# Four transformer blocks on one core: the first two tiles of x in one load, the first weights on one queue in halves, and five instruction lists put in a new order

## The chip, the cores and the metric

The kernel runs on one core of a Trainium2 chip. The metric is the device time of one execution in microseconds. Before the change three runs took 328.64, 327.99 and 327.65 us; the median is 327.99.

A core has a matrix engine (PE), three engines for elementwise work (DVE, the vector engine; ACT, the scalar engine; POOL, GpSimd) and a queue engine (SP) that only starts transfers here. PE multiplies a weight tile of 128x128 with a moving tile of up to 512 columns and writes to PSUM, of which there are eight banks of 128x512 float32. The engines run their own instruction streams and wait for each other on semaphores.

## The reference

x has 2048 rows of 512 columns. Two kinds of block follow each other twice:

```python
def _A_ref(x, wqkv, wo):                # H = 32 heads of Dh = 16
    qkv = (x @ wqkv).reshape(B, S, 3, H, Dh).transpose(2, 0, 3, 1, 4)
    q, k, v = qkv[0], qkv[1], qkv[2]
    phi = lambda t: jnp.where(t > 0, t + 1, jnp.exp(t)) + 1e-6
    pq, pk = phi(q), phi(k)
    kv = jnp.einsum("bhsd,bhse->bhde", pk, v)
    z = jnp.einsum("bhsd->bhd", pk)
    num = jnp.einsum("bhqd,bhde->bhqe", pq, kv)
    den = jnp.einsum("bhqd,bhd->bhq", pq, z)[..., None] + 1e-6
    return (num / den).transpose(0, 2, 1, 3).reshape(B, S, D) @ wo

def _B_ref(x, w1, b1, w2, b2):          # F = 1792
    y = _layernorm(x)
    h = _gelu(jnp.einsum("bsd,df->bsf", y, w1) + b1)
    return jnp.einsum("bsf,fd->bsd", h, w2) + b2

x = x + _A_ref(_layernorm(x), wqkv, wo)
x = x + _B_ref(_layernorm(x), w1, b1, w2, b2)
x = x + _A_ref(_layernorm(x), wqkv, wo)
x = x + _B_ref(_layernorm(x), w1, b1, w2, b2)
```

The attention is linear: kv and z are sums over all rows, so no row's output can be made before all rows' K have been seen.

## The kernel before

**Tiles and chunks.** The rows are cut into 16 tiles of 128 rows and 4 chunks of four tiles. In the first attention the chunks are taken in the order 3, 0, 1, 2, so the first tiles are 12 and 13. All weights stay in SBUF.

**Names.** The kernel builds a graph of operations, each of which is one or a few instructions, and every operation has a name made of its kind, the layer (0 or 1), and the tile or chunk. For a tile of x: `stats`, `aggr`, `veps`, `pow`, `nmr` and `norm` are the steps of the layernorm (for the very first tiles `cen` subtracts the mean and `ysc` scales later, and tile 13 takes its sum and its sum of squares on ACT: `sumA0_13`, `sqA0_13`, `negA0_13`, L722 to L731). The normalized tile is transposed, either on PE (`PT`, L797, with a copy `tc` from PSUM, L807) or by a transposing DMA that SP starts (`TA` and `TB`, L784; `TP`, L1069, for the attention's output). `K` (L852) and `Q` (L870, L883) are the projections, `phik` and `phiq` their feature map, which is made of `exp`, `relu` and `min`. `G` (L953, L985) sums phi(k) times the normalized rows, `Z` sums phi(k); `gt` and `ga` collect G from PSUM on DVE, and from it `KV` (L1008) makes kv and `M` (L1031) joins it with wo. `D` (L1077) gives the denominators, then come `den`, `rec` and the product `pr` (L1065). `WO` (L1101) is the output projection, `RA` (L1106) its residual add. `W1` (L1133) with `gelu` (L1139) on ACT and `W2` (L1171, the last tile in two halves at L1158) are the two matrices of the second block, `RB` (L1177, L1181) its residual add, `OD` (L1183, L1165) the store of a tile of the result. `W10_1_3_0` is W1 in layer 0, chunk 1, third block of 128 of the 1792 features, first part.

**What sets the order.** Each engine plays a list of operation names that is written out in the configuration: 388 names for PE, 323 for ACT, 506 for DVE, 220 for POOL, 104 for SP. Which engine does an operation is fixed in another table. A planner, `Scheduler.run`, replays the five lists with modelled durations: from its times it takes only which buffer slot or PSUM bank a tile gets, and with that which semaphores an operation waits for. It does not change the order in a list. An operation whose inputs are late holds up all that stands behind it in its engine's list; this holds for SP too, where a transpose that waits for its tile holds up the transposes and stores behind it.

**The loads at the start.** SP starts, in this order, `x0` (128 KB, tile 12, L648), `x1` (128 KB, tile 13, L650), `wk0` (the upper half of the K weights, 256 KB, L657), `x2` (256 KB, tiles 14 and 15, L650), `wq` (512 KB, L660) and the three other chunks of x (`xc0` to `xc2`, 512 KB each, L644). ACT starts `wk1`, the lower half of the K weights, as the first operation of its list. POOL starts the loads of wv, wo, w1 and w2 in pieces of up to 896 KB later on, in places of its own list. Behind x and wk come the first matmuls: PE transposes tile 12 and tile 13, with dummy matmuls (L690) before and between, and does `K0_12` and `K0_13`, then tile 14's transpose and the first Q projection `Q0_3_0`.

Of the kernel before, what the change touches and what calls it, by code (L numbers as in the profile page):

```python
# [7 lines left out]
ACT = mybir.ActivationFunctionType  # L8
ALU = mybir.AluOpType

P = 128
# [16 lines left out]
DMA_LAT = 800.0  # L28

# [81 lines left out]
class Scheduler:  # L111
# [12 lines left out]
    def run(self):  # L124
# [13 lines left out]
        bus = 0.0  # L138
        for _ in g.ops:
            best = None  # L140
            for e in ENGINES:
                if len(self.order[e]) == len(queue[e]):
                    continue
                o = queue[e][len(self.order[e])]
                if o.missing:
                    continue
                at = max(o.ready, free[e])
                if o.table is not None and o.table != table:
                    at = max(o.ready, free[e] + TABLE_LOAD)
                slots = [self.slot_time(t) for t in o.tiles if t.slot is None]  # L150
# [20 lines left out]
            if o.fast:  # L171
                dve_busy = at + dur
            if e == "pool" and o.sem is None and o.dur > 300.0:
                dur += max(0.0, min(dve_busy - at, 400.0))
                pool_busy = at + dur
# [92 lines left out]
def assign_waits(graph, order, sems, dma_sems):  # L268
# [10 lines left out]
    while len(done) < total:  # L279
        moved = False  # L280
        for e in ENGINES:
# [43 lines left out]
    N_WARM2=1, N_IDLE=[4, 3], XQ='sp', WKQ='sp act', WK1=1,  # L325
    LAND={'x0': 3210, 'x1': 3930, 'wk1': 5300, 'wk0': 6430, 'x2': 6950, 'wq': 8450, 'xc0': 9730, 'xc1': 11020, 'xc2': 12240},
# [1041 lines left out]
```

## Time and profile before

| what | us |
|---|---|
| median of three runs | 327.99 |
| the profiled execution, first to last instruction | 326.2 |
| PE busy | 320.6 |
| DVE busy | 218.7 |
| ACT busy | 197.5 |
| POOL busy | 131.2 |
| x0, x1, wk1, wk0, x2, wq landed at | 3.18, 4.76, 5.53, 6.24, 6.94, 8.41 |

The profile gives the profiled execution from its first to its last instruction only: 326.2 us, which is 1.8 us less than the median of the timed runs. A matmul's busy time covers its way through the array, in which the next one already starts, so the busy time of PE hides some pauses of a few tenths; they are seen in the starts of the instructions and in the waits of the weight loads (PEld). Chain lines say what the end hung on, step by step backwards. A row of the timeline has a start, a duration, the engine, the line, and in square brackets the idle time before it with what ended it. A stretch row has the busy time of each engine with its number of instructions, the granted clock, the share of the DMA engines and the rate in GB/s.

### The profile page before, as it was taken

Reading aid. Unit: us, or ns where it says so; the run is one execution under the profiler, and the core shown is the slowest. Engines: PE = TensorE matmul, PEld = TensorE weight load, DVE = VectorE, ACT = ScalarE, POOL = GpSimd, SP = SyncE. Lnnn points to the kernel's source line nnn. Section 1 sums busy time; section 2 is a strip of 40 time slices with the busy share of each in tenths; the row PEclk is TensorE's granted clock in tenths of the full one; section 3 lists DMA queues with packets and bytes.
Section 4 is the critical chain, followed back from the end, with each engine's and each line's share of the span. In section 5 each row is a group of like instructions: output and inputs, shape, how many; then the busy total and the mean of one; then the engine's idle time right before and its main releaser. Section 6 shows DMA issues by size and latency. Waiting matters only on the chain.

```text
span 326.2 us, 4796 instructions
## 1 busy us (share of the span) xinstructions
PE 320.6 (98%) x1724; PEld 158.2 (48%) x1724; DVE 218.7 (67%) x506; ACT 197.5 (61%) x338; POOL 131.2 (40%) x224
## 2 busy tenths in 40 slices
PE   7999999999999999999999999999999999999996
PEld 3444545656544444444444444458644444444453
DVE  4998689989866662535468899999988663300132
ACT  5998889744753387357963395969923553645200
POOL 3465637673238106134139525645811275100000
PEclk9999999999999999999999999999999999999999
DMA  7424662524012400312110200111153233300011
GB/s 239 163 51 92 173 223 62 181 49 81 21 31 48 97 1 2 74 22 55 27 32 19 47 17 0 28 39 36 32 92 72 48 45 69 81 0 2 32 64 50
DMA packets 47028, 20.39 MB, mean 62 GB/s; under 512 B 41948, under 2 KB 45532, under 8 KB 47004
## 3 DMA queue, kind: packets, MB, share of 16 engines
q1 hardware_dynamic: 45676, 15.09, 20.4%
q0 software_dynamic: 1056, 4.72, 4.5%
q10 hardware_dynamic: 272, 0.26, 0.3%
q8 instruction: 14, 0.23, 0.3%
q14 instruction: 10, 0.08, 0.1%
HBM read 8.00 MB, written 2.10 MB: 31 GB/s over the span
## 4 chain that ended last, share of the span: by engine, by line
PE 91%; DVE 4%; DMA 2%; ACT 1%; SPq 1%; issue 1%; ACTq 0%
PE ps L1133 29%; PE ps L1171 26%; PE ps L1101 9%; PE ps L852 9%; PE ps L870 5%; PE ps L953 4%; PE ps L883 3%; PE ps L985 2%; DMA t<-in_A_x_dram 1%; PE ps L1158 1%; DMA t<-yb 1%; DVE t L839 1%; PE ps L1008 1%; PE ps L1077 1%; PE ps L797 1%
## 5 line engine op out<-in xcount | busy, mean ns | idle before, releaser
L1139 ACT ACTIVATE gT<-ps,b1c 128x512 bf16<-128x512 f32 (+1 forms) x140 | 76.9, 601 | 61.2 <-PE ps L1133 60.8
L1133 PE MATMUL ps<-t,w 128*128 128x512 bf16 (+1 forms) x560 | 102.2, 336 | 0.5 <-DMA t<-yb 0.3
L1171 PE MATMUL ps<-w,gT 128*128 128x512 bf16 x434 | 97.3, 379 | 0.0
L1133 PEld LDWEIGHTS ps<-t,w 128*128 128x128 bf16 x560 | 54.4, 98 | 44.5 <-DMA t<-yb 0.7
L1171 PEld LDWEIGHTS ps<-w,gT 128*128 128x128 bf16 x434 | 42.4, 98 | 50.4 <-ACT gT L1139 0.3
L822 ACT ACTIVATE eb<-ps 128x512 bf16<-128x512 f32 x56 | 32.1, 606 | 21.3 <-PE ps L852 20.3
L749 POOL TENSOR_TENSOR rstd<-veps,neghalf 128x1 f32<-128x1 f32 x64 | 36.7, 581 | 8.2 <-DVE veps L747 5.5
L1181 DVE TENSOR_TENSOR outb<-ps,xsb 128x512 bf16<-128x512 f32 x15 | 10.3, 689 | 40.3 <-PE ps L1171 32.1
L734 DVE BATCH_NORM_STATS2 stats<-xsb 128x6 f32<-128x512 f32 x48 | 32.0, 681 | 0.2
L1101 PE MATMUL ps<-gtb,t 128*128 128x512 bf16 x128 | 31.8, 379 | 0.1
L852 PE MATMUL ps<-wqkv,t 128*128 128x512 bf16 x128 | 31.1, 379 | 0.0
L769 ACT ACTIVATE yb<-xsb,nmr,rstd 128x512 bf16<-128x512 f32 x21 | 16.8, 811 | 12.6 <-POOL nmr L766 12.5
L833 ACT ACTIVATE rb<-ps 128x512 bf16<-128x512 f32 x38 | 22.3, 611 | 1.6 <-PE ps L852 0.9
L739 POOL TENSOR_SCALAR veps<-mv 128x1 f32<-128x1 f32 x32 | 7.3, 227 | 38.4 <-DVE mv L736 36.6
L774 DVE TENSOR_SCALAR yb<-xsb,mv,rstd 128x512 bf16<-128x512 f32 x27 | 15.0, 572 | 9.0 <-POOL rstd L749 8.9
L835 DVE TENSOR_SCALAR eb<-eb 128x512 bf16<-128x512 bf16 x46 | 13.6, 306 | 10.9 <-ACT eb L822 10.8
L1118 POOL TENSOR_TENSOR xsb<-xsb,b2b 128x512 f32<-128x512 f32 x14 | 17.0, 1218 | 8.1 <-DVE yb L774 6.5
L870 PE MATMUL ps<-wqkv,t 128*128 128x512 bf16 x80 | 20.2, 379 | 0.0
L747 POOL TENSOR_SCALAR veps<-mv 128x1 f32<-128x1 f32 x28 | 8.4, 305 | 28.0 <-DVE mv L736 26.9
L1101 PEld LDWEIGHTS ps<-gtb,t 128*128 128x128 bf16 x128 | 12.3, 98 | 14.9 <-ACT gtb L966 0.7
L852 PEld LDWEIGHTS ps<-wqkv,t 128*128 128x128 bf16 x128 | 12.0, 97 | 14.7 <-ACT t L807 0.9
L1065 POOL TENSOR_TENSOR t<-t,rr 128x512 bf16<-128x512 bf16 x7 | 7.7, 1100 | 24.4 <-DVE rr L1061 14.1
(103 smaller groups left out, 398.7 us busy)
## 6 DMA issues: line engine op xcount, KB each, us to landing
w<-in_B_w_dram POOLq DMA_DIRECT2D x4, 896.0 KB, 5.9
out_dram<-outb SPq DMA_DIRECT2D x15, 128.0 KB, 2.1
t<-in_A_x_dram SPq DMA_DIRECT2D x3, 512.0 KB, 7.3
t<-yb SPq DMA_TRANSPOSE x56, 2.5
wqkv<-in_A_wqkv_dram SPq DMA_DIRECT2D x1, 512.0 KB, 5.7
wo<-in_A_wo_dram POOLq DMA_DIRECT2D x1, 512.0 KB, 6.6
wqkv<-in_A_wqkv_dram POOLq DMA_DIRECT2D x1, 512.0 KB, 4.5
t<-t SPq DMA_TRANSPOSE x20, 2.5
```

The costliest lines, as they stand in the source:

```text
L734: G.op("dve", lambda e: e.bn_stats(stats[:, s.slot, :], src()), 620, reads=src_keys, writes=[k + "s"], tiles=[s, *src_tiles], prio=prio, n ...
L749: G.op("pool", lambda e: e.tensor_tensor(rstd[:, s.slot:s.slot + 1], veps[:, s.slot:s.slot + 1], neghalf[:], op=ALU.pow), 570, reads=[k + ...
L769: G.op("act", lambda e: e.activation(yb[:, y.slot, :], src(), ACT.Identity, bias=nmr[:, s.slot:s.slot + 1], scale=rstd[:, s.slot:s.slot + 1]),
L822: G.op("act", lambda e: e.activation(eb[:, et.slot, :], bank(bt), ACT.Exp, scale=factor()), 478, reads=[src_key, *more], writes=[f"e{tag}" ...
L833: G.op("act", lambda e: e.activation(rb[:, rt.slot, :], bank(bt), ACT.Relu, scale=factor()), 478, reads=[src_key, *more], writes=[f"r{tag} ...
L852: ins = e.matmul(bank(b), lhsT=yTa(yT)[:, dt, k * P:(k + 1) * P], rhs=wqkv[:, dt, D:2 * D], start=(dt == 0), stop=(dt == DT - 1))
L870: ins = e.matmul(bank(b), lhsT=yTa(yT)[:, dt, k * P:(k + 1) * P], rhs=wqkv[:, dt, 0:D], start=(dt == 0), stop=(dt == DT - 1))
L1101: ins = e.matmul(bank(wb), lhsT=yTa(pq)[:, kt, k * P:(k + 1) * P], rhs=gtb[:, kt, :], start=(kt == 0), stop=(kt == DT - 1))
L1118: G.op("pool" if on_pool else "dve", lambda e: e.tensor_tensor(xsb[:, st, :], xsb[:, st, :], b2b[:], op=ALU.add), 1120 if on_pool else 600 ...
L1133: ins = e.matmul(bank(b, n), lhsT=w1[:, dt, ft * P:(ft + 1) * P], rhs=yTa(yT)[:, dt, k0 * P:k1 * P], start=(dt == 0), stop=(dt == DT - 1))
L1139: G.op("act", lambda e, ft=ft, b=b, k0=k0, k1=k1, n=n: e.activation(gT[:, g.slot, ft * 512 + k0 * P:ft * 512 + k1 * P], bank(b, n), ACT.Ge ...
L1171: ins = e.matmul(bank(b), lhsT=gT[:, g.slot, ft * 512 + k * P:ft * 512 + (k + 1) * P], rhs=w2[:, ft, :], start=(ft == 0), stop=(ft == FT - 1))
```

## The change

1. **The first loads.** `x0` and `x1` become one load named `x0` of both tiles (256 KB, each partition 2 KB in a row of memory). `wk1` is started by SP instead of ACT. SP's order becomes `x0 wk0 wk1 x2 wq xc0 xc1 xc2`; ACT's list loses `wk1`.
2. **The first two K projections.** `K0_12` and `K0_13` become two operations of two matmuls each. The first (`K0_12_0`) waits for the upper half of the K weights alone, the second for the lower.
3. **The planner's model.** Durations and latencies of many operations are set anew, POOL gets a turnaround between kinds of instructions, a transposing DMA that follows another kind of transfer on SP is modelled as starting at least 620 ns after it and one right behind another transpose as 75 ns longer, and the interplay of DVE and POOL is modelled in another way. The landing times that are assumed for the first loads are set anew.
4. **The lists.** All five lists are put in a new order. The names in them are the same but for `x1` (gone), `wk1` (from ACT's to SP's) and the two new `K0_12_0` and `K0_13_0`. The engine of each operation stays. In the new order ACT switches between its function tables 18 times instead of 14.

The diff, cut to its core; of the lists only some stretches are shown, and durations are shown by example:

```diff
-    N_WARM2=1, N_IDLE=[4, 3], XQ='sp', WKQ='sp act', WK1=1,
-    LAND={'x0': 3210, 'x1': 3930, 'wk1': 5300, 'wk0': 6430, 'x2': 6950, 'wq': 8450, 'xc0': 9730, 'xc1': 11020, 'xc2': 12240},
+    N_WARM2=1, N_IDLE=[4, 3], XQ='sp', WKQ='sp sp', WK1=0, K_SPLIT=2, K_SPLIT0=0,
+    LAND={'x0': 3440, 'wk0': 4320, 'wk1': 5080, 'x2': 6600, 'wq': 8500, 'xc0': 9800, 'xc1': 11100, 'xc2': 12350},
...
-        dma("sp", lambda e: e.dma_start(x0ap(HC, 0), rows(x_dram, HC)[:, 0, :]), [("x0", FIRST)], [x0[HC]], prio=-120, name="x0", kb=128)
-        for k, n in ((1, 1), (2, 2)):
+        for k, n in ((0, 2), (2, 2)):
             dma(cf["XQ"], lambda e, k=k, n=n: e.dma_start(
                 t4[:, x0[HC].slot, k * D:(k + n) * D].rearrange("p (k d) -> p k d", k=n), rows(x_dram, HC)[:, k:k + n, :]),
...
+            if L == 0 and c == HC and k < cf["K_SPLIT"]:
+                halves = tuple(range(cf["K_SPLIT0"], len(cf["WKQ"].split()))) + tuple(range(cf["K_SPLIT0"]))
+                for i, h in enumerate(halves):
+                    def part(e, h=h, i=i):
+                        n = DT // len(halves)
+                        for j in range(n):
+                            ins = e.matmul(bank(b), lhsT=yTa(yT)[:, n * h + j, k * P:(k + 1) * P], rhs=wqkv[:, n * h + j, D:2 * D],
+                                           start=(i == j == 0), stop=(i == len(halves) - 1 and j == n - 1))
+                        return ins
...
+                if e == "sp" and last is not None and o.name[0] == "T" and last.name[0] != "T" and last.nbytes >= 0:
+                    at = max(at, last.start + 620.0)
...
-            if o.fast and pool_busy > at:
-                dur += pool_busy - at - 60.0
+            if e == "sp":
+                if last is not None and o.name[0] == last.name[0] == "T" and at - free[e] < 30.0:
+                    dur += 75.0
+                last = o
...
-                 570, reads=[k + "v", "neghalf"], writes=[k + "r"], tiles=[s], prio=prio, name=f"pow{tag}")
+                 530, reads=[k + "v", "neghalf"], writes=[k + "r"], tiles=[s], prio=prio, name=f"pow{tag}", lat=50)
```

Stretches of the lists, before and after:

```text
PE, start     before: warm PTA0_12 idle0_0 PTA0_13 idle0_1 K0_12 K0_13 PTA0_14 Q0_3_0 Q0_3_2 PTA0_15 K0_14
              after:  warm PTA0_12 idle0_0 PTA0_13 idle0_1 K0_12_0 K0_12 K0_13_0 K0_13 PTA0_14 Q0_3_0 Q0_3_1 K0_14
SP, TB0_5     before: TB0_1 TB0_2 TB0_3 TB0_5 TB0_6 TB0_7 TB0_4 TP0_2_1
              after:  TB0_2 TB0_4 TB0_6 TP0_3_1 TP0_2_0 TB0_7 TB0_5 TP0_2_2
DVE, normB0_5 before: statsB0_4 statsB0_6 normB0_2 normB0_3 normB0_5 aggrB0_6
              after:  red0_2_1 RB0_0 pz0_2_2 normB0_5 red0_2_2
PE, KV1       before: G1_3_3 G1_3_0 G1_2_3 Q1_3_0 KV1_0 KV1_1 Q1_3_1 KV1_2 D1_0_3 Q1_3_2 KV1_3
              after:  Q1_3_1 G1_2_3 D1_0_2 G1_3_3 KV1_0 Q1_3_2 D1_0_3 KV1_1 KV1_2 KV1_3
SP, TP1_3_0   before: TP1_3_3 TP1_3_2 OD0 TP1_3_0 TP1_2_0
              after:  TB1_3 TP1_3_1 TB1_5 TP1_3_0 TB1_4
SP, TB1_15    before: TB1_12 TB1_14 OD2 TB1_13 TB1_15 OD4
              after:  OD2 TB1_14 TB1_12 TB1_15 TB1_13 OD3
DVE, pr1_2_2  before: rec1_2_2 RA1_12 rec1_2_1 RA1_8 pr1_2_2
              after:  statsB1_14 aggrB1_14 aggrB1_12 b21_7 pr1_2_2
```

POOL starts its late loads before in the order w2_0, wo, wv, w1_0, w1_1, w2_1 and after in the order w1_0, wo, w1_1, wv, w2_0, w2_1.

More of the change, by code (lines that the diff above doesn't have):

```diff
@@ L28 @@
 DMA_LAT = 800.0
+FORM = {"vepsA": 1, "vepsB": 2, "nmr": 3}
+TURN = ((0.0, 115.0, 115.0, 15.0), (0.0, 0.0, 120.0, 135.0), (0.0, 0.0, 0.0, 15.0), (0.0, 120.0, 120.0, 15.0))
 class Pool:
@@ L138, in run @@
         bus = 0.0
+        last = None
+        form = 0
         for _ in g.ops:
@@ L647, in build_kernel @@
         ones = G.op("dve", lambda e: e.memset(onesm[:], 1.0), 480, writes=["onesm"], prio=-300, name="ones", lat=0)
-        dma("sp", lambda e: e.dma_start(x0ap(HC, 0), rows(x_dram, HC)[:, 0, :]), [("x0", FIRST)], [x0[HC]], prio=-120, name="x0", kb=128)
-        for k, n in ((1, 1), (2, 2)):
+        for k, n in ((0, 2), (2, 2)):
             dma(cf["XQ"], lambda e, k=k, n=n: e.dma_start(
                 t4[:, x0[HC].slot, k * D:(k + n) * D].rearrange("p (k d) -> p k d", k=n), rows(x_dram, HC)[:, k:k + n, :]),
-                [("x0", FIRST + k + i) for i in range(n)], [x0[HC]], prio=-119, name=f"x{k}", kb=128 * n,
-                after=[ones] if cf["XQ"] == "act" and k == 1 else ())
+                [("x0", FIRST + k + i) for i in range(n)], [x0[HC]], prio=-119, name=f"x{k}", kb=128 * n)
         wsp = cf["WKQ"].split()
@@ L821, in factor @@
                 return rstd[:, by[0].slot:by[0].slot + 1] if by else 1.0
-            G.op("act", lambda e: e.activation(eb[:, et.slot, :], bank(bt), ACT.Exp, scale=factor()), 478, reads=[src_key, *more], writes=[f"e{tag}"],
+            G.op("act", lambda e: e.activation(eb[:, et.slot, :], bank(bt), ACT.Exp, scale=factor()), 569 if by else 483, reads=[src_key, *more], writes=[f"e{tag}"],
                  tiles=[bt, et, *held], prio=prio, name=f"exp{tag}", lat=90, table="exp")
@@ L854, in fn @@
                 return ins
-            G.op("pe", fn, 4 * MM, reads=[f"yT{L}_{st}", "wk"], writes=[f"k{L}_{st}"], tiles=[b, yT], prio=prio,
-                 name=f"K{L}_{st}", lat=MM_DRAIN, n=4, after=after)
+            if L == 0 and c == HC and k < cf["K_SPLIT"]:
[7 more added lines that the diff above has]
+                        return ins
+                    G.op("pe", part, DT // len(halves) * MM, reads=[f"yT{L}_{st}", f"wk_{h}"] + ([f"k{L}_{st}"] if i else []), writes=[f"k{L}_{st}"],
+                         tiles=[b, yT], prio=prio, name=f"K{L}_{st}" + (f"_{i}" if i < len(halves) - 1 else ""), lat=MM_DRAIN, n=DT // len(halves), after=after)
+            else:
+                G.op("pe", fn, 4 * MM, reads=[f"yT{L}_{st}", "wk"], writes=[f"k{L}_{st}"], tiles=[b, yT], prio=prio,
+                     name=f"K{L}_{st}", lat=MM_DRAIN, n=4, after=after)
             phi(b, f"k{L}_{st}", lambda: pkb[:, pk.slot, :], f"pk{L}_{st}", [pk], prio, f"k{L}_{st}", by)
```

48 lines of the change are left out of this document (27 added, 21 removed), and 275 rows, old and new, of the table ORDER.

## The prediction

> **What bounds the kernel now.** I read the page's busy shares first, then the chain that ended last, the stretches of time, and the timeline at PE's pauses.
>
> ```profile
> PE 320.6 (98%) x1724; PEld 158.2 (48%) x1724; DVE 218.7 (67%) x506; ACT 197.5 (61%) x338; POOL 131.2 (40%) x224
> PEclk9999999999999999999999999999999999999999
> PE 91%; DVE 4%; DMA 2%; ACT 1%; SPq 1%; issue 1%; ACTq 0%
> ```
>
> PE is busy 98% of 326.2 us at full granted clock, and the diff leaves its matmuls alone: same number, same shapes. So the time moves only by PE's pauses. Adding up each 512-column matmul at 0.216 us start to start (a gapless run: 7.77 us for 36) and the narrower ones likewise, PE's work is about 317.3 us from its first instruction; the last matmul group starts 6.2 us later than this work alone would put it. 4.1 of these 6.2 are there when the first Q projection starts at 8.67, 2.3 gather afterwards. That 2.3 and a part of the head are all that can be won.
>
> The stretches (start:end, PE, PEld, DVE, ACT, POOL, clock, DMA):
>
> ```profile
> 4.00:8.50 4.50, 3.18 (x26) 1.61 (x25) 2.65 (x10) 3.28 (x8) 1.46 (x3) 1.00 1.07 386
> ...
> 80.00:130.00 50.00, 50.00 (x242) 23.41 (x240) 31.57 (x71) 28.70 (x42) 18.40 (x36) 1.00 0.16 33
> 130.00:160.00 30.00, 30.00 (x141) 13.58 (x140) 13.67 (x30) 18.12 (x26) 8.04 (x18) 1.00 0.24 49
> ...
> 200.00:215.00 15.00, 14.71 (x80) 6.68 (x78) 14.63 (x37) 10.94 (x21) 10.67 (x13) 1.00 0.14 28
> ```
>
> PE pauses at 4 to 8.5, where the DMA engines are full; from 80 to 160 it never does, whatever the lists do there; at 200 to 215 DVE is full and PE waits for it. The pauses in the timeline:
>
> ```profile
> 0.80 0.40 SPq L648 DMA_DIRECT2D t<-in_A_x_dram  x1
> 1.25 0.42 SPq L650 DMA_DIRECT2D t<-in_A_x_dram  x1
> ...
> 3.21 0.69 DVE L734 BATCH_NORM_STATS2 stats<-t 128x6 f32<-128x512 bf16 x1 [1.76 <-DMA t<-in_A_x_dram]
> ...
> 4.78 0.63 ACT L722 ACTIVATE eb<-t 128x512 bf16<-128x512 bf16 x1 [2.71 <-DMA t<-in_A_x_dram]
> ...
> 6.13 0.23 PEld L797 LDWEIGHTS ps<-idp,yb 128*128 128x128 bf16 x4 [1.12 <-DVE veps L747]
> ...
> 8.68 0.59 PE L870 MATMUL ps<-wqkv,t 128*128 128x512 bf16 x2
> ```
>
> Tile 12 starts when x0 lands (3.18), tile 13 when x1 lands (4.76); the first Q projection starts 0.26 after wq lands (8.41).
>
> ```profile
> 78.81 0.59 PE L1133 MATMUL ps<-t,w 128*128 128x512 bf16 x2 [0.25 <-issue]
> ...
> 206.12 0.23 PEld L1008 LDWEIGHTS ps<-gtb,wqkv 128*128 128x128 bf16 x4 [0.52 <-DVE gtb L998]
> ...
> 272.07 0.55 PEld L1133 LDWEIGHTS ps<-t,w 128*128 128x128 bf16 x4 [0.75 <-DMA t<-yb]
> ```
>
> These are the three largest pauses afterwards: counted on matmul starts, W10_1 loses 0.41 at 78.8 (its last transpose TB0_4 landed at 78.72), KV1_0 0.43 at 206.1, W11_3 0.42 at 272.1. The rest are K0_14 to Z0_1 0.51 together (before 50 us), KV1_3 0.19, WO1_1 and WO1_12 0.38.
>
> **The change, part by part.** The sum is made against the profiled 326.2 us. The runs' median, 327.99, lies 1.8 above this span; I take 1.8 to stay.
>
> *Head.* x0 and x1 become one load of 256 KB; wk1 leaves ACT's queue and is third on SP's, so SP still issues wq fifth (at 2.69) and the later x loads behind it. The pair's landing is not in the trace. Lower bound 3.18 (as x0); the next 128 KB at wq's rate (512 KB in 1.47 us, 6.94 to 8.41) gives 3.18 + 0.37 = 3.55; upper bound about 4.0, half-way to x1's 4.76. I take 3.4, since the pair is in the descriptor stream first and has no rival. Tile 12's transpose came 1.39 after landing, so 4.8 instead of 4.57; tile 13's comes at about 5.4 instead of 6.13, since its sum on ACT need not wait until 4.76. K0_12 then starts at about 5.9 instead of 6.54: 0.65 won. But next in line are x2 (landed 6.94) and wq (8.41), both behind the same 1.5 MB: K0_13 ends at 7.6, PE waits for tile 14 and then for wq. Only 0.12 to 0.17 of the 0.65 is left at the first Q. I take -0.15. Bounds: between 2.75 and 4.0 us the engines moved 23 to 46 KB per quarter of a microsecond against 82 and more later, some 290 KB or 0.7 us at the full rate lost; if that dip belongs to the two queues, wq comes 0.7 earlier (-0.85); if two loads of wk in a row lose as much again, +0.5. Splitting K0_12 and K0_13 in halves adds no matmul. The 768 KB up to the end of wk landed at 6.24 before, 512 KB of them at 5.53; if the halves land so again, the first starts at 5.9 and the second wants wk1 at 6.33: just covered. Without the split K0_12 would wait 0.3 longer, and the wait for wq would swallow that too, so the split is worth 0 (at most 0.3).
>
> A rule bears on that bound. The Trainium skill ("DMA: Bandwidth & Descriptors", section "Issuing engines are not separate DMA queues") says that loads started by different engines run interleaved on the same 16 DMA engines, and that several issuers only save issuing time. By that rule the dip stays and wq lands at 8.4; the low rate with two issuers in the trace allows the other reading.
>
> *Early lists (to 50 us).* By the order of the lists and the rows' durations, DVE's phik0_13 comes 1.26 us later (end 12.8, G0_13 wants it at 13.05), tcA0_15 is moved on ACT (13.5, K0_15 at 13.9), normA0_4 is 2.95 later on DVE (0.1 to 0.2 of slack before K0_4). I take 0.3 lost instead of 0.51: -0.2 (-0.5 to +0.3).
>
> *W10_1.* The first matmul group to need a late transpose is now W10_1_13_0, 2.2 us of PE work later in PE's list (10 more 512-column matmuls ahead). Its last transpose TB0_5 is behind TP0_3_1, TP0_2_0 and TB0_7 on SP and its normB0_5 behind RB0_0 on DVE; at 1.25 us a transpose on SP it lands at about 78.6 for a need at 80.2. -0.41; bounds -0.41 and +0.2 (a transpose that waits as TB0_4 did, 3.98 from issue to landing).
>
> *KV1.* 0.86 us of PE work is moved ahead of KV1_0: its 0.43 goes. gt1_3 has the same DVE work ahead (0.04 less) and DVE is full, so KV1_3 is late next, by 0.3 to 0.5 instead of 0.19. -0.25 (-0.62 to +0.6, one DVE operation of 0.6).
>
> *WO1.* TP1_3_0 is issued ahead of OD0, so WO1_12's 0.28 goes; but pr1_2_2 comes 3.44 us later on DVE, and TP1_2_2 lands at 257.2 for WO1_10 at 257.4. -0.2 (-0.38 to +0.5).
>
> *W11_3.* TB1_15 waited on SP behind an out store (1.51 us) and 2.49 us of flight; now all four transposes are ahead of it with some 2.8 us in hand. -0.42; bounds -0.42 and 0.
>
> *Elsewhere.* ACT gets 4 more table loads of 1.28 us, mostly at 130 to 160, where it is busy 18.1 of 30: 5.1 us beside 11.9 idle, hidden if no gelu's result is wanted within 1.3; by my walk W20_12 has 1.6. w2_1 is issued later by POOL (about 60.8, landing in 5.95 us at 66.7, needed at 67.75). W21_3 and K1_14 have 0.1 to 0.2. For such places that become late I add +0.5 (0 to +1.5). On SP the stores OD change places only with transposes above.
>
> Sum: -0.15 - 0.2 - 0.41 - 0.25 - 0.2 - 0.42 + 0.5 = -1.13; 326.2 - 1.1 + 1.8 = 326.9. Measuring tells about 0.3% (0.98 us) from no change.
>
> **Rivals.**
> (1) *Hidden.* The pauses wander: the same full DVE and the same SP queue feed the same matmuls, and each pause removed appears at the next tight place (four are named above with 0.1 to 0.2 in hand). For: 200 to 215, DVE 14.63 of 15. Against: W11_3 and W10_1 have over 1 us in hand. Then the new places cost as much as W10_1, KV1 and WO1 give (0.86) besides the 0.5: 327.0 to 328.4, about 327.8.
> (2) *Slower: POOL holds DVE.* DVE's 128x512 product beside POOL's took 1.21 us at 74.82 and 1.22 at 250.65 against 0.61 to 0.69 alone; the 128x32 add at 75.95 took 1.13 against 0.17, ending 0.04 after POOL's operation. With DVE full from 171 to 236, each such meeting costs PE 0.56 to 0.96 there. The new lists place these operations anew and may bring more meetings (or fewer). Four more at 0.75 are +3.0: 326.9 + 3.0 = 329.9. To pass 329.0, (329.0 - 326.9)/0.75 = 2.8, so three more decide it. The Trainium skill ("Advanced Engine Details and Errata", "Mode Summary") has the rule: the second vector port is shared with GpSimd, and they block each other. These rows agree.
> (3) *Head.* The dip vanishes with ACT's load: wq 0.7 earlier, 326.2. Or the pair lands no earlier than x1 did (4.76): K0_12 as late as before, wq unmoved, 327.1: the change would not do at the head what it says.
>
> **How the numbers follow.** Forecast (pauses fall by 1 to 2 us, 326.0 to 327.0): 0.48, in which case 3's early wq has 0.08. Rival 1: 0.30, in which case 3's late pair has 0.08. Rival 2 and any other of its sign: 0.22. So faster by over 0.3% (below 327.0) 0.48, within 0.3% 0.30, slower 0.22. Range: with all pauses after the head gone it is 328.0 - 2.3 - 0.15 = 325.6; I go to 325.8. Upwards rival 2 with two to three more meetings, 329.4, leaves some 0.15 out. The likeliest case's own range is 326.0 to 327.5.
>
> **What would show it.** Right: x's first landing at 3.2 to 3.6, second transpose near 5.4, first Q at 8.5 to 8.6; no pause at W10_1 and W11_3, KV1_0's gone and KV1_3's still there; the last matmul group 1 us earlier. Wrong: wq late (after 8.9); DVE's products at 1.2 us more often between 171 and 236; a pause of over 0.5 us at G0, K0_4, W20_12, W20_1, WO1_10 or W21_3.

## The result, and the profile after

The changed kernel takes 328.77 us (median of seven runs, 328.48 to 329.82) against 327.65 (327.39 to 328.64) for the kernel before on the same chip: a ratio of 1.0035 with a 95% interval of 1.0022 to 1.0047. That is 1.1 us slower where 1.1 us faster was forecast. The profiled execution took 328.69 us with a span of 327.0, so 1.7 us lie around the span (1.8 before).

The page's busy shares and chain, and two stretches (start:end, length, PE, PEld, DVE, ACT, POOL, clock, DMA):

```profile
PE 318.3 (97%) x1693; PEld 158.7 (49%) x1724; DVE 218.8 (67%) x506; ACT 203.4 (62%) x342; POOL 134.3 (41%) x224
...
PE 81%; DVE 9%; DMA 4%; POOL 2%; ACT 2%; issue 1%; SPq 1%; DVEq 0%; ACTq 0%
```

```profile
4.00:8.50 4.50, 3.83 (x29) 1.78 (x27) 3.09 (x11) 3.43 (x9) 1.31 (x3) 1.00 0.91 318
...
200.00:215.00 15.00, 14.95 (x82) 7.28 (x82) 14.81 (x37) 11.46 (x22) 12.61 (x14) 1.00 0.14 28
```

This trace lacks 31 of PE's 1724 matmul records (all weight loads are there), so PE's busy time reads some 2 us lower than before with the same work. I filled the gaps by the known order of the matmuls and compared starts. PE is busier at 4 to 8.5 (3.83 against 3.18), and at 200 to 215 PE no longer waits for DVE. The three large pauses shown before are gone: W10_1, KV1 and W11_3 lose nothing. Others stand in their place. Four of PE's waits in the profile after:

```profile
PE ps L1192 <- ACT gT L1160: 0.8, 1, 0.8
PE ps L861 <- DMA t<-yb: 0.6, 1, 0.6
PE ps L806 <- DVE stats L734: 0.5, 1, 0.5
PE ps L891 <- DMA wqkv<-in_A_wqkv_dram: 0.4, 1, 0.4
```

These are, from below, the first Q projection (wq landed at 8.79), tile 12's transpose at 4.97, K0_11 at 33.3 (0.72 late on matmul starts) and W21_3 at 238.4 (0.98 late). And there is a place that no wait of PE shows, the end. Its timeline, of the changed kernel:

```profile
318.71 0.69 DVE L1202 TENSOR_TENSOR outb<-ps,xsb 128x512 bf16<-128x512 f32 x1 [3.84 <-PE ps L1192]
319.43 4.80 SPq L1204 DMA_DIRECT2D out_dram<-outb  x2
320.24 0.42 DVE L1184 TENSOR_TENSOR outb<-ps,xsb 128x256 bf16<-128x256 f32 x1 [0.84 <-PE ps L1179]
323.18 0.69 DVE L1202 TENSOR_TENSOR outb<-ps,xsb 128x512 bf16<-128x512 f32 x1 [2.51 <-DMA out_dram<-outb]
323.79 0.41 DVE L1184 TENSOR_TENSOR outb<-ps,xsb 128x256 bf16<-128x256 f32 x1
```

There are two output buffers. Tile 11's add at 323.18 waits 2.51 us for a buffer, until the store of tile 10, issued at 319.43, has landed at 323.09. In the trace's packets an instruction load (a packet of the kind "instruction", which brings an engine a piece of its program) of 16 KB starts at 320.39 and takes 1.52 us; the other parts of the store had begun to land at 321.11. Tile 15's second half stands behind tile 11 on DVE and on SP. So PE's last matmul starts at 322.97, 0.41 us earlier than before (323.38), and the end comes 3.99 us after it instead of 2.84.

The table sets the profiled executions side by side, with those of the experiments below. "Q" is the start of the first Q projection, "lost after" what PE loses from there to its last matmul, "end" the time from the start of the last matmul to the end of the span. "K0_11, Z0_2" are the pauses of PE ahead of these two, near 33 and 39 us; the old lists have another order there.

| kernel | x's first landing | tile 12's transpose | Q | lost after | K0_11, Z0_2 | end | span |
|---|---|---|---|---|---|---|---|
| before | 3.18 | 4.57 | 8.67 | 2.37 | | 2.84 | 326.2 |
| before, again | 3.21 | 4.59 | 8.43 | 2.51 | | 2.84 | 326.1 |
| changed | 3.59 | 4.97 | 8.84 | 1.86 | 0.72, 0 | 3.99 | 327.0 |
| changed, again | 4.04 | 5.42 | 8.91 | 2.00 | 0.78, 0.62 | 4.14 | 327.4 |
| changed, tile 15 in a free buffer | 4.23 | 5.61 | 10.45 | 2.61 | 0.79, 0.53 | 2.84 | 328.2 |
| changed, W21_3's gelus first | 4.03 | 5.42 | 9.24 | 1.71 | 0.77, 0.55 | 3.89 | 327.1 |
| changed, normA0_11 earlier | 3.97 | 5.35 | 10.50 | 1.43 | 0.13, 0 | 2.85 | 327.1 |
| changed, first loads as before | 3.54 | 4.92 | 8.73 | 1.61 | 0.13, 0 | 3.86 | 326.5 |
| changed, x0 and x1 apart | 3.21 | 4.59 | 9.86 | 2.73 | 0.78, 0.55 | 2.84 | 327.7 |
| changed, wk1 on ACT | 3.66 | 5.04 | 8.91 | 2.88 | 0.78, 0.54 | 2.84 | 326.9 |
| changed, no split | 3.58 | 4.96 | 9.24 | 2.61 | 0.79, 0.54 | 2.84 | 327.0 |
| changed, three narrow dummies more | 3.56 | 4.94 | 9.16 | 2.61 | 0.79, 0.53 | 4.05 | 328.1 |
| changed, 11 dummies | 4.36 | 5.74 | 9.28 | 0.72 | 0.13, 0 | 4.27 | 326.6 |
| changed, 11 dummies, tile 15 in a free buffer | 3.44 | 4.99 | 8.77 | 0.76 | 0.13, 0 | 4.15 | 326.0 |
| before, new first loads | 3.58 | 4.96 | 8.70 | 3.13 | | 2.87 | 327.0 |
| before, new first loads, 11 dummies | 3.46 | 5.58 | 9.12 | 2.45 | | 2.83 | 326.7 |
| four edits | 3.18 | 4.56 | 8.49 | 0.88 | 0.13, 0 | 2.83 | 324.5 |

### The profile page after: what moved, and what is told of

It is laid out like the page before. It is cut to its first block, busy times and chain, and to the rows that moved or that the text cites. A ratio compares the mean times of both kernels' runs of the same rounds, so it can differ in the third digit from the quotient of the medians.

```text
span 327.0 us, 4777 instructions
## 1 busy us (share of the span) xinstructions
PE 318.3 (97%) x1693; PEld 158.7 (49%) x1724; DVE 218.8 (67%) x506; ACT 203.4 (62%) x342; POOL 134.3 (41%) x224
## 4 chain that ended last, share of the span: by engine, by line
PE 81%; DVE 9%; DMA 4%; POOL 2%; ACT 2%; issue 1%; SPq 1%; DVEq 0%; ACTq 0%
PE ps L1192 26%; PE ps L1154 25%; PE ps L861 7%; PE ps L1122 6%; PE ps L1006 4%; PE ps L974 4%; PE ps L891 4%; PE ps L904 3%; DMA wqkv<-in_A_wqkv_dram 2%; DVE stats L743 2%; DVE xsb L1127 2%; POOL rstd L758 1%; DMA out_dram<-outb 1%; DMA t<-yb 1%; DVE t L848 1%
## 5 line engine op out<-in xcount | busy, mean ns | idle before, releaser
L758 POOL TENSOR_TENSOR rstd<-veps,neghalf 128x1 f32<-128x1 f32 x64 | 38.7, 609 | 6.4 <-DVE veps L756 4.3
L861 PE MATMUL ps<-wqkv,t 128*128 128x512 bf16 x118 | 28.6, 379 | 0.7 <-DMA t<-yb 0.6
L783 DVE TENSOR_SCALAR yb<-xsb,mv,rstd 128x512 bf16<-128x512 f32 x27 | 15.8, 585 | 10.2 <-POOL rstd L758 10.1
L891 PE MATMUL ps<-wqkv,t 128*128 128x512 bf16 x80 | 20.1, 379 | 0.5 <-DMA wqkv<-in_A_wqkv_dram 0.4
L1198 DVE TENSOR_TENSOR xsb<-ps,xsb 128x512 f32<-128x512 f32 x16 | 10.9, 684 | 11.5 <-PE ps L1192 11.5
L861 PEld LDWEIGHTS ps<-wqkv,t 128*128 128x128 bf16 x120 | 11.3, 98 | 14.7 <-DVE eb L835 1.0
```

The source lines that it names most:

```text
L758: G.op("pool", lambda e: e.tensor_tensor(rstd[:, s.slot:s.slot + 1], veps[:, s.slot:s.slot + 1], neghalf[:], op=ALU.pow), 530, reads=[k + ...
L861: ins = e.matmul(bank(b), lhsT=yTa(yT)[:, dt, k * P:(k + 1) * P], rhs=wqkv[:, dt, D:2 * D], start=(dt == 0), stop=(dt == DT - 1))
L891: ins = e.matmul(bank(b), lhsT=yTa(yT)[:, dt, k * P:(k + 1) * P], rhs=wqkv[:, dt, 0:D], start=(dt == 0), stop=(dt == DT - 1))
```

## The experiments

Every ratio is against the kernel before, run beside it on the same chip. The median of before lies between 327.65 and 328.91 from one set of runs to the next, so ratios are compared, not times. A profile is one execution; the ratio is of many. In the diffs, lines of the configuration and of the lists are cut at both ends; where first loads are put back or taken over, the lines that issue them and the landing times that the planner assumes go with them and are not shown.

**The changed kernel again.** No edit.

> The changed kernel, unaltered, beside the others on the same chip. Theory: the first Q projection starts between 8.8 and 10.5, varying from execution to execution; ratio to before 1.002 to 1.006 and a spread of the runs of over 1.5 us. Rival: 1.0035 with a spread as small as that of the kernel before, so that the first loads' landing is no cause of spread.

Measured: 1.0024 (1.0008 to 1.0040), runs from 328.91 to 330.98, a spread of 2.1 us. The spread came, and the first Q of this execution at 8.91. Before's 31 runs beside it spread by 2.4, so spread alone tells nothing here.

**First loads as before.**

```diff
-    N_WARM2=1, N_IDLE=[4, 3], XQ='sp', WKQ='sp sp', WK1=0, K_SPLIT=2, K_SPLIT0=0,
+    N_WARM2=1, N_IDLE=[4, 3], XQ='sp', WKQ='sp act', WK1=1, K_SPLIT=2, K_SPLIT0=0,
...
-            "x0 wk0 wk1 x2 wq xc0 xc1 xc2 TA0_0
+            "x0 x1 wk0 x2 wq xc0 xc1 xc2 TA0_0
...
-            "sumA0_13 tcA0_12 tcA0_13 sqA0_13
+            "wk1 sumA0_13 tcA0_12 tcA0_13 sqA0_13
```

> The changed kernel with the first loads as before: x0 and x1 apart, wk1 started by ACT; the split of K0_12 and K0_13 stays. Theory: the new first loads bring wq later (8.79 against 8.41), so the first Q projection starts at about 8.67 instead of 8.84 and the time falls by 0.1 to 0.2 us, or stays. Rival: the new first loads are worth their early K projections: the time rises by 0.3 us or more.

Measured: 0.9963 (0.9947 to 0.9980): 1.2 us faster than before, and 0.6 to 0.7% under the changed kernel. My theory put the first loads at 0.1 to 0.2 us; they are worth about ten times that. What remains of the change, the lists and the split, is a gain of 1.2 us (0.7 to 1.7).

**New first loads in the kernel before.** The same edit the other way: one load for the pair, both halves of wk on SP; lists as before.

> The kernel before with the new first loads alone: x0 and x1 as one load, wk0 and wk1 on SP; lists, model and the unsplit K projections as before. Theory: the new first loads are the largest single loss of the change: the first Q projection starts 0.2 to 0.6 us later, or 1.8 later where the matmuls run at half rate, so the time is 0.5 to 1.5 us over that of before (ratio 1.0015 to 1.005). Rival: the loads alone are worth a small gain or nothing and the lists are what loses: ratio 0.998 to 1.001.

Measured: 1.0038 (1.0022 to 1.0053). The first loads alone lose 1.2 us, with the old lists as well. Its profiled execution, 328.78 us, is the shortest of its twelve runs (median 329.52), and the first Q was at 8.70 in it: one execution was not enough to see the loss. Of the 0.89 us by which its last matmul comes later than in the second profile of before, 0.27 are there at the first Q and 0.42 come at W11_3.

**Half rate.** Two experiments that were meant for other places showed what happens in other executions. The timeline of the changed kernel with normA0_11 moved, at the start:

```profile
2.92 1.59 PE L699 MATMUL ps<-const-bfloat16-1.0 128*128 128x512 bf16 x4
3.99 0.69 DVE L743 BATCH_NORM_STATS2 stats<-t 128x6 f32<-128x512 bf16 x1 [2.54 <-DMA t<-in_A_x_dram]
5.35 0.61 PE L806 MATMUL ps<-idp,yb 128*128 128x128 bf16 x4 [0.84 <-DVE stats L734]
...
6.92 3.51 PE L870 MATMUL ps<-wqkv,t 128*128 128x512 bf16 x8
...
10.28 0.39 PE L806 MATMUL ps<-idp,yb 128*128 128x128 bf16 x4
10.50 0.81 PE L891 MATMUL ps<-wqkv,t 128*128 128x512 bf16 x3
```

The eight matmuls of K0_12 and K0_13 take 3.51 us, where they take 1.90 in the profile after: seven of the eight are followed by the next start after 0.427 us; from the first Q on it is 0.216. In every profile the dummies at the start are 0.427 apart at first; here PE stays at half rate until about 9.9. The pair landed at 3.97, the dummies were done at 4.51, and PE stood idle for 0.84 us before tile 12's transpose. The execution with tile 15 in a free buffer did the same (landed 4.23, idle for 1.10, six matmuls at 0.427, Q at 10.45). A stretch's granted clock reads 1.00 in all of this, because the trace's record of the clock has no entry ahead of the first full-rate one. That first entry is at 10.20 here, at 4.69 in the profile after and at 3.90 in the changed kernel's second one, as the starts say.

The Trainium skill ("TensorE: Matmul & The Clock Gate", section "What's actually happening") says that PE runs at half clock until a free-running window of about 3.4 us has been busy, and that the point of the change therefore varies from run to run. The traces agree: the same first loads gave half rate until 9.8 and 9.9 in two executions, and K projections at full rate in the profile after. In the fifteen traces with such a record the full rate lasts for 317.44, 320.85 or 324.27 us, in steps of 3.41. In the 3.41 us ahead of the first entry PE was busy for at least 2.91 in all fifteen; the two such windows before it in this trace, which end at 3.38 and 6.79, have 2.55 and 2.57. The idle 0.84 us lie in the second.

Half rate is not the whole loss. K0_12 and K0_13 ran at half rate in two of the nine profiles that have the pair as one load and eight wide dummies. In the seven of these that have all of the new first loads and no further dummies, the first Q starts at 9.41 on the mean, against 8.58 in the four profiles with the old first loads; 0.42 of these 0.83 us come from the two at half rate, 0.41 from later starts in the others.

**More dummies.**

```diff
-    C0=(3, 0, 1, 2), N_WARM=8, ZC=(0, 3), LQ='sp',
+    C0=(3, 0, 1, 2), N_WARM=11, ZC=(0, 3), LQ='sp',
```

> The changed kernel with 11 instead of 8 wide dummy matmuls ahead of tile 12's transpose; nothing else. Theory: with the new first loads the pair lands late (3.6 to 4.2 in four profiles), PE stands idle from 4.25 to 5.0 or 5.6, and in some executions its matmuls then run at half rate (0.427 us for 512 columns) until about 10, so that the first Q projection starts at 10.5 instead of 8.8 to 9.2. Three more dummies (0.65 us at full rate, 1.28 at half) fill the idle time: no matmul of K0_12 or K0_13 at 0.427, first Q at 8.8 to 9.2, and the time falls by 0.3 to 1.2 us against the changed kernel, with less spread. Rival: the dummies only push the first transposes back by up to 0.5 us and the rate does not depend on them: same time or up to 0.5 us longer.

Measured: 0.9979 (0.9962 to 0.9996), on the chip where the changed kernel took 1.0024: 1.2 us of median less (328.0 against 329.22). No matmul of K0_12 or K0_13 at 0.427, first Q at 9.28. In these two profiles the gain is not at the first Q, which is 0.37 later than in the changed kernel's second one; PE lost only 0.72 after Q instead of 2.00. Two of PE's waits there, of the changed kernel's second profile, are gone:

```profile
PE ps L861 <- DMA t<-yb: 0.6, 1, 0.6
PE ps L955 <- DVE zs L964: 0.5, 1, 0.5
```

These are K0_11, whose pause fell from 0.78 to 0.13, and Z0_2, whose 0.62 went; W21_3's is 0.30 in both. So the dummies might have helped by moving things along PE's program. Two more kernels bear on this.

**Three narrow dummies instead of three wide ones.**

```diff
-    N_WARM2=1, N_IDLE=[4, 3], XQ='sp',
+    N_WARM2=4, N_IDLE=[4, 3], XQ='sp',
```

> The changed kernel with three more narrow dummies (128 columns, 0.06 us each at full rate, 0.11 at half) ahead of tile 12's transpose: PE's program is as much longer as with 11 wide dummies, but PE is busy only 0.17 to 0.33 us longer. Theory A (the wide dummies help by keeping PE busy until the pair has landed): no help here, ratio to before as the changed kernel, 1.002 to 1.0035. Theory B (they help by moving the instruction loads along PE's program, away from the transposes of K0_11 and from what W21_3 waits for): same help, ratio 0.997 to 0.999, K0_11's pause 0.1 and W21_3's 0.3.

Measured: 1.0028 (1.0015 to 1.0041), K0_11's pause 0.79, Z0_2's 0.53, W21_3's 0.98: no help. PE's program is as long as with the wide ones, so its length is not what helps. But this run does not show that it is the time in which PE is busy: K0_12 and K0_13 ran at full rate here too, and the pauses at K0_11 and Z0_2, which the wide dummies remove, stayed.

**New first loads and 11 dummies in the kernel before.**

> The kernel before with the new first loads (as in the run with these alone) and 11 wide dummies. Theory A (PE idle ahead of the late pair is the loss): ratio to before 1.000 to 1.002, 0.5 us or more under the 1.0038 without the dummies. Theory C (the first loads lose by landing x2 and wq late, whatever PE does): 1.003 to 1.0045 again.

Measured: 1.0000 (0.9990 to 1.0009). The whole loss of 0.38% (measured on another chip) is gone, although the pair still lands at 3.46 and the first Q of this execution, the longest of its twelve, is at 9.12. The start of its timeline:

```profile
2.92 2.87 PE L688 MATMUL ps<-const-bfloat16-1.0 128*128 128x512 bf16 x7
3.48 0.69 DVE L732 BATCH_NORM_STATS2 stats<-t 128x6 f32<-128x512 bf16 x1 [2.03 <-DMA t<-in_A_x_dram]
5.59 0.56 PE L795 MATMUL ps<-idp,yb 128*128 128x128 bf16 x4
5.98 0.39 PE L688 MATMUL ps<-const-bfloat16-1.0 128*128 128x128 bf16 x4
```

The dummies last until the transpose, which has no wait in brackets. The old lists have no pause at K0_11 to lose, so here the dummies help in another way. That they keep PE busy fits, but the profile without them shows no half rate beyond 6.23 either, so how they bring back 1.2 us in most executions stays open.

**The kernel before again.**

> The kernel before, unaltered, with a profile from the same chip as the two others. Theory: x0 lands between 3.2 and 3.6, the first Q projection starts at 8.5 to 8.8, never at half rate; the end follows the last matmul group's start by 2.85 us; ratio 1.000. Rival: the head of the kernel before varies as much as that of the changed one (first Q later than 9.2), and the head is no difference between them.

Measured: 0.9995 (0.9984 to 1.0005), x0 at 3.21, first Q at 8.43, end 2.84. Its transposes and first dummies between them run at half rate (0.61 us for four narrow matmuls), but K0_12 and K0_13 take 1.89 us.

**Which part of the first loads.** In one kernel x0 and x1 apart, wk on SP; in the other the pair as one load, wk1 on ACT.

```diff
-            "x0 wk0 wk1 x2 wq xc0 xc1 xc2 TA0_0
+            "x0 x1 wk0 wk1 x2 wq xc0 xc1 xc2 TA0_0
...
-            "x0 wk0 wk1 x2 wq xc0 xc1 xc2 TA0_0
+            "x0 wk0 x2 wq xc0 xc1 xc2 TA0_0
-            "sumA0_13 tcA0_12 tcA0_13 sqA0_13
+            "wk1 sumA0_13 tcA0_12 tcA0_13 sqA0_13
```

> The changed kernel with x0 and x1 as two loads again, and both halves of wk on SP as in the change. Theory A: the pair's landing is what costs (it lands at 3.6 to 4.4 where x0 alone lands at 3.2 to 3.5, and PE stands idle until tile 12's transpose): with x0 alone first, tile 12's transpose comes at 4.6 to 4.95, the matmuls of K0_12 never run at half rate, and the time falls by 0.7 to 1.5 us against the changed kernel (ratio to before 0.996 to 1.000). Theory B: the queue is what costs (wk1 on SP moves x2 and wq back); then this kernel stays at the changed kernel's 1.002 to 1.0035.

> The changed kernel with x's pair as one load, but wk1 started by ACT as before. Theory A (the pair's landing costs): tile 12's transpose still at 5.0 or later, ratio to before 1.002 to 1.0035 as the changed kernel. Theory B (the queue costs): wq lands 0.3 to 0.5 earlier, first Q before 8.7, ratio 0.996 to 1.000.

Measured: 1.0040 (1.0025 to 1.0055) and 1.0009 (0.9997 to 1.0021). Neither theory holds alone. With x0 apart tile 12's transpose came early (4.59), yet x2 landed at 8.25 and wq at 9.68, and the first Q was at 9.86, with PE at full rate from 4.45. So wk1 on SP costs something without any half rate. With wk1 on ACT the pair still came late (3.66, transpose at 5.04) and wq landed no earlier (8.79), yet this kernel is better than the changed one by about 0.2%. Only both together give 0.9963. In the packets, each of the kernels with one of the new parts or both falls to 25 to 61 KB per quarter of a microsecond at some point between 4.5 and 6.5 us (42 to 46 at 5.0 to 6.0 in the profile after); those with x0 and x1 apart and wk1 on ACT have their low stretch at 2.75 to 4 and run at 84 and more from 4.25 on. What makes this low stretch stays open: the trace does not say which DMA engine a packet was on.

**No split.** K0_12 and K0_13 as one operation each.

```diff
-    WKQ='sp sp', WK1=0, K_SPLIT=2, K_SPLIT0=0,
+    WKQ='sp sp', WK1=0, K_SPLIT=0, K_SPLIT0=0,
...
-            "warm PTA0_12 idle0_0 PTA0_13 idle0_1 K0_12_0 K0_12 K0_13_0 K0_13 PTA0_14
+            "warm PTA0_12 idle0_0 PTA0_13 idle0_1 K0_12 K0_13 PTA0_14
```

> The changed kernel without the split: K0_12 and K0_13 as one operation each, waiting for both halves of wk. Theory: worth nothing to 0.2 us: K0_12 starts when wk1 has landed, at 6.0 to 6.3 (7.0 in the latest landings), and PE waits for tile 14 and wq behind it in any case; first Q unmoved, ratio to before 1.002 to 1.004. Rival: the later K projections leave PE idle longer ahead of them and the half rate comes more often: 0.5 us or more over the changed kernel.

Measured: 1.0030 (1.0018 to 1.0042), as the changed kernel. The split is worth nothing that can be measured here, with an interval of 0.12% to each side.

**W21_3.** In ACT's list:

```diff
-  gelu1_0_10_0 expq1_2_3 normB1_4 normB1_7 normB1_6 gelu1_0_9_1 gelu1_0_3_1 gelu1_0_2_1 expq1_2_2 gelu1_1_1_0
+  gelu1_0_10_0 gelu1_0_9_1 gelu1_0_3_1 gelu1_0_2_1 expq1_2_3 normB1_4 normB1_7 normB1_6 expq1_2_2 gelu1_1_1_0
```

> The changed kernel, with gelu1_0_9_1, gelu1_0_3_1 and gelu1_0_2_1 ahead of expq1_2_3 and the three normalizations in ACT's list, and expq1_2_2 behind them, which also takes two function table loads away. Theory: W21_3's pause of 0.98 us at 238.4 is ACT's order (three gelus behind two table loads and the late nmrB1_7); it goes, PE's total loss falls from 5.25 to about 4.3, and the time falls by 0.8 to 1.0 us. Rival: W21_3 then waits for something else, or WO1_12 or W11_1_1 two places on takes the pause over, as expq1_2_3 and normB1_4 come 1.4 us later: the time falls by less than 0.3 us.

In the profile after, the timeline reads:

```profile
234.34 1.52 ACT L778 ACTIVATE yb<-xsb,nmr,rstd 128x512 bf16<-128x512 f32 x2 [1.37 <-POOL nmr L775]
...
235.87 1.28 ACT L1325 ACT_TABLE_LOAD   x1
...
237.17 1.21 ACT L1160 ACTIVATE gT<-ps,b1c 128x256 bf16<-128x256 f32 x3
...
238.43 0.82 PE L1192 MATMUL ps<-w,gT 128*128 128x512 bf16 x3 [0.82 <-ACT gT L1160]
```

ACT waits 1.37 us for POOL, loads its table, makes three gelus, and W21_3 starts when the third is done. With the gelus first:

```profile
231.81 4.70 PE L1192 MATMUL ps<-w,gT 128*128 128x512 bf16 x21
...
237.20 2.97 PE L1192 MATMUL ps<-w,gT 128*128 128x512 bf16 x13
```

The pause is gone and none follows in its place. The time is 1.0018 (1.0002 to 1.0035) against 1.0024 and 1.0035: it does not show 0.8 to 1.0 us. So much was to be had only in some executions: of the profiles with the old order the pause is 0.95 to 0.98 in most, but 0.30 in the changed kernel's second one and in both with 11 dummies. And this execution had a pause of 0.55 at Z0_2 that the profile after does not have, but six others do. There DVE's small operations took 0.95 and 0.59 instead of 0.29, while POOL issued weight loads and made a mask (in the profile after the first took 0.95 as well, the second 0.27):

```profile
36.71 0.95 POOL L683 DMA_DIRECT2D w<-in_B_w_dram  x1
...
37.09 0.95 DVE L835 TENSOR_SCALAR eb<-eb 128x512 bf16<-128x512 bf16 x1
...
37.97 0.59 DVE L844 TENSOR_SCALAR eb<-eb 128x512 bf16<-128x512 bf16 x1
...
38.46 1.14 POOL L689 TENSOR_SCALAR_AFFINE_SELECT bdmask<-bdmask 128x512 bf16<-128x512 bf16 x1
```

**K0_11.** In DVE's list:

```diff
-  minq0_0_2 minq0_3_3 phiq0_3_3 normA0_11 mink0_5
+  minq0_0_2 normA0_11 minq0_3_3 phiq0_3_3 mink0_5
```

> The changed kernel, with normA0_11 two places earlier in DVE's list, in an idle time of 0.8 us. Theory: K0_11's pause of 0.72 us at 33.3 is the late transpose TA0_11 (issued at 30.11, landed 3.08 later, 0.6 of that behind an instruction load of 8 KB); issued 0.5 us earlier it lands at about 32.1, and the pause falls to under 0.1: the time falls by 0.5 to 0.7 us. Rival: the transpose is met by the instruction load at any place or the next transpose, TA0_9, takes the pause over: less than 0.2 us.

Measured: the pause fell from 0.72 to 0.13, and the ratio is 0.9986 (0.9971 to 1.0001), in spite of half rate in the profiled execution. But the pause is also 0.13 in three kernels without this edit (first loads as before, and both with 11 dummies). What divides them is an instruction load of 8 KB: in the profile after it starts 1.72 us after TA0_11 is issued and the transpose takes 3.08 us to land; in four executions with a start at 1.72 or 1.73 it took 3.1, in four with a start at 2.16 to 2.43 it took 2.47 to 2.55. Half a microsecond decides whether they meet.

The table shows more than this one edit. All eight profiles of the new lists with one or both of the new first loads, and with neither 11 dummies nor this edit, have the load at 1.72 or 1.73 and a pause of 0.72 to 0.79; the five others of the new lists have it at 2.16 to 2.43 and 0.13. Z0_2's pause of 0.53 to 0.62 is in seven of the eight and in none of the five. So this edit took away two pauses, 1.2 us together where both stand, and its ratio is 0.3 to 0.5% (1.0 to 1.6 us) under the kernels with all of the new first loads that have them (1.0016 to 1.0035). That is more than half of the 0.5 to 0.7% by which the first loads as before help. How often the pauses come, one profile of each kernel does not show: the kernel with wk1 on ACT has both in its profile and still 1.0009. Why the first loads and the dummies move the instruction load against the transpose stays open.

**The end.** Tile 15's result in a buffer of the normalized tiles, alone and with 11 dummies.

```diff
-                ot = Tile(OUT, f"out{st}")
+                ot = Tile(YB, f"out{st}")
...
-   e.tensor_tensor(outb[:, ot.slot, cs], bank(hb, D // 2), xsb[:, st, cs], op=ALU.add)
+   e.tensor_tensor(yb[:, ot.slot, cs], bank(hb, D // 2), xsb[:, st, cs], op=ALU.add)
```

> The changed kernel, with the last tile's result (tile 15) put into a free buffer of the normalized tiles instead of one of the two output buffers. Theory: at the end the residual add of tile 11 waits 2.51 us for the store of tile 10 (issued at 319.43, landed at 323.09, its last packets behind an instruction load of 1.5 us), and tile 15's second half is behind it on DVE and on SP. With the buffer free, RB1_11 follows W21_11 at about 322.0, RB1_15_1 follows the last matmul group at 323.3, and the end comes 0.7 to 1.1 us earlier: span about 326.0, ratio to before about 1.000. Rival: the last store's own flight sets the end, or the next store is late in the same way; then the span stays within 0.3 of the changed kernel's 327.0.

> The changed kernel with the first loads as in the change, 11 wide dummies, and tile 15's result in a free buffer. Theory: where an instruction load of 16 KB meets the store of tile 10 at about 320, the kernels with two output buffers need 3.9 to 4.3 us from the last matmul's start to the end; with the buffer free it is 2.85, met or not. The time falls by 0.5 to 1.2 us against the kernel with 11 dummies alone (ratio to before 0.994 to 0.997). Rival: the end is as late as without the buffer when the load is met (over 3.5 us): the buffer was not what held it.

Measured: 1.0016 (0.9998 to 1.0034) and 0.9994 (0.9983 to 1.0005). The first profile was no test: no instruction load fell into its last stores, and the end took 2.84. The execution with normA0_11 earlier had none there either, and with two buffers as in the change its end took 2.85 (three more such took 2.83 to 2.84); tile 11's add waited for PE, not for a store:

```profile
319.99 0.69 DVE L1202 TENSOR_TENSOR outb<-ps,xsb 128x512 bf16<-128x512 f32 x1 [3.84 <-PE ps L1192]
...
323.03 0.69 DVE L1202 TENSOR_TENSOR outb<-ps,xsb 128x512 bf16<-128x512 f32 x1 [1.08 <-PE ps L1192]
```

In the second, the load came at 323.22 and met the very last store, which landed at 325.49 after a first part at 324.01: an end of 4.15, with a buffer free. So the rival stands: the load makes the end late. A buffer could help where the load meets an earlier store, which neither run showed. In six executions with the changed end and a load at 319.8 to 321.5 the end took 3.86 to 4.27. In the kernel before the load comes as well (320.08) and meets the store of tile 8, for which nothing behind it has to wait long: 2.84.

**Four edits together.** First loads as before, tile 15's buffer, W21_3's gelus, normA0_11.

> The changed kernel with four edits together: the first loads as before, tile 15's result in a free buffer, the three gelus of W21_3 ahead of the exponentials, and normA0_11 earlier. Theory: the losses add up, so their removal does: against the changed kernel the head gives 1 to 2 us on the mean, the end 1.1, W21_3 1.0, K0_11 0.1 to 0.6; the time falls to 2 to 3 us under that of before (ratio 0.991 to 0.994), span about 324.5. Rival: a pause removed reappears a few operations later, and the ratio stays at 0.996 or above, as with the first loads alone.

Measured: 0.9950 (0.9932 to 0.9968), 327.13 us against 328.34 for before; faster than both kernels, by 0.5% and, on the same chip, 0.7%. The span of its profiled execution is 324.5, but that execution took 327.38, 2.9 more than the span where the other profiled ones have 1.7 to 2.3, so the ratio and not the span tells the gain. (The medians of the spans, 324.5 of eight runs against 326.5, differ by 2.0.) The waits of PE in its profile:

```profile
PE ps L700 <- PEq L1375: 0.8, 1, 0.8
PE ps L807 <- DVE veps L757: 0.4, 1, 0.4
```

No wait of a quarter of a microsecond is left after tile 13's transpose. The theory's 2 to 3 us were 1.6; the rival's bound of 0.996 lies inside the interval, so how much the three edits add to the first loads (0.9963 alone, on another chip) is not settled.

## Why the prediction was wrong, point by point

- **Head: the failed step.** "I take -0.15" for the new first loads, with +0.5 as the upper bound. Measured: they cost 0.38% (1.2 us) with the old lists and 0.5 to 0.7% (some 2 us) with the new; at the first Q it was +0.17 in the profiled execution and +1.8 in two of the profiles. "I take 3.4" for the pair's landing was at the good end: it landed at 3.44 to 4.36 in twelve profiles, beyond my upper bound of 4.0 in four. I held wq to be unmoved; it landed at 8.15 to 9.24 in the eleven profiles with all of the new first loads, against 7.90 to 8.69 in four with the old. I carried every delay of tile 12 as time hidden by the wait for wq and never asked what PE does meanwhile. The row was there: the dummies' 3.37 us for nine in the profile before, 0.427 apart, twice the 0.216 of all later ones. PE came to full rate only at 3.76 and was idle for 0.37 us ahead of tile 12's transpose; the change makes this 0.5 to 1.15. And I took the head's worth to end at the first Q, where with the new lists K0_11 and Z0_2, 25 and 30 us later, pause for 0.7 to 1.4 us with the new first loads and for 0.13 with the old. How the 1.2 us with the old lists divide is not known.
- **The dip** did not belong to the two queues. With all of wk on SP it came back at 5 to 6 us and wq landed 0.38 later. The rule of the Trainium skill cited there ("DMA: Bandwidth & Descriptors", section "Issuing engines are not separate DMA queues") would have kept the dip, and the trace agrees as far as that; that leaving ACT's queue costs something, as 1.0009 with wk1 on ACT against 1.0030 without (same chip, one without the split) suggests, does not follow from it.
- **The split: right.** Worth 0; 1.0030 without it.
- **Early lists: right sum for the old pauses, wrong for the new.** K0_14 to Z0_1 lost 0.51 and now nothing, but K0_11 0.72, and Z0_2 0.5 to 0.6 in most other profiles, places I had not named; I had looked at K0_4.
- **W10_1 and W11_3: right**, both gone (-0.41, -0.42). **KV1 and WO1: better than forecast**, gone altogether but for 0.1 at WO0 (-0.62 and -0.28, against -0.25 and -0.2). The lists with the old first loads are 1.2 us faster than before; steps after the head had summed to -0.98. That these are near each other is partly luck, as the steps themselves were off both ways.
- **Elsewhere: mis-sized.** +0.5 taken, 0.98 at W21_3 (named, "0.1 to 0.2" in hand) and 0.72 at K0_11.
- **The end: not in the sum.** I wrote that the stores change places only with transposes; the order of the last stores and adds had changed too, and it cost 1.15 in the profiled execution (3.99 - 2.84), where an instruction load met a store; without such a load the changed end takes 2.84 as well.
- **The sum.** PE's last matmul is 0.41 us earlier than before, not 1.13; with the end, +0.7 us of span, and over the runs +1.1. (The two parts of the pauses before, 4.1 and 2.3, make 6.4 and not the 6.2 that I wrote; no term hangs on it.)
- **The rivals.** The slower one was the wrong mechanism. From 171 to 236 DVE's products do not last longer: mean 678 ns of five in the profile after, against 736 of four before. The row of the profile after:

```profile
L1086 DVE TENSOR_TENSOR t<-t,rr 128x512 bf16<-128x512 bf16 x5 | 3.4, 678 | 0.0
```

DVE's operations were longer beside POOL's at Z0_2, which paused for 0.5 to 0.6 in seven profiles; no run tests that POOL is the cause. Pauses came up in new places as the first rival has it, but the time was not the 327.8 of that rival, and it named neither K0_11 nor the end.

The two effects do not add up: 0.9963 for the lists and 1.0038 for the first loads would make 1.000, and the changed kernel has 1.0024 to 1.0035, 0.8 to 1.1 us more. The pauses at K0_11 and Z0_2, which only the new lists with new first loads have, are of this size. The intervals are 0.15 to 0.17% to each side and the chips differ, so the match is not exact.

## What to carry to other kernels

Ask of every change at a kernel's start what PE does while it waits: some tenths of a microsecond of idle time cost nothing by themselves, but the first Q came 1.6 us later in two of nine profiles in which they fell before PE had come to full rate. Make dummy matmuls last until the first real one in the latest landing, not in the one profile at hand. Do not end the account of a head at the first matmul that waits for data: here more than half a microsecond was lost 25 us later, where a transpose met an instruction load. And where pauses depend on landings that vary by half a microsecond from execution to execution, a sum made in tenths from one trace is good for the direction of each step, not for the sign of a total of 0.3%.

## What the runs showed of the hardware

- The same load of 256 KB, first in the queue, landed at 3.44 to 4.36 us from execution to execution; the load of 128 KB at 3.18 to 3.54.
- Single instruction loads of 8 or 16 KB took 0.3 to 1.7 us and made a transpose land 0.6 us late (3.1 instead of 2.5) or an output store 1.3 to 2 us late, when they met it.
- 512-column matmuls started 0.427 us apart until the first full-rate entry of the trace's clock record, which came at 3.74 to 10.20 us, and 0.216 apart after it. Ahead of that entry the stretch rows read a clock of 1.00 all the same.
- That entry came only at the end of a 3.41 us window in which PE had been busy for 2.91 us or more (fifteen traces); windows with 2.57 or less did not bring it.
